# Two early loads issued by ScalarE's queue: a token tile and the scale columns of an adaptive layernorm

## The chip, the cores and the metric

The kernel runs on one core of a Trainium2 chip. A core has TensorE (PE, with its weight loads shown as PEld), VectorE (DVE), ScalarE (ACT), GpSimd (POOL) and SyncE (SP). Each engine works through its own instructions in program order and waits on semaphores for the others. SyncE and ScalarE can issue DMA transfers; each of the two has a queue of its own, and the 16 DMA engines of the core move the data of both. The metric is the device time of one execution in microseconds (us).

## The reference, cut to what matters

A token sequence `x` of 2048 x 512 goes through an attention block and a token-mixing MLP, each behind a layernorm whose scale and shift come from a condition vector `c` of 512 numbers:

```python
mod = (_silu(c) @ w_mod).reshape(c.shape[0], 6, 1, -1)
sa, ca, ga, sb, cb, gb = (mod[:, i] for i in range(6))
h = _layernorm(x, axis=-1) * (1 + ca) + sa
x = x + ga * _A_ref(h, A_wqkv, A_wo)      # sliding, dilated local attention, 32 heads
h = _layernorm(x, axis=-1) * (1 + cb) + sb
x = x + gb * _B_ref(h, B_w1, B_b1, B_w2, B_b2)   # MLP over the token axis
```

`w_mod` is 512 x 3072; its columns 512 to 1023 give `ca`, the scale of the first modulation. All inputs and the output are bf16.

## The kernel before

The 2048 tokens are 16 tiles of 128 rows (`xx[:, st, :]`), worked in chunks of 2, 4, 4, 4 and 2 tiles. Every operation is entered into a graph with a name, an engine (or several to choose from), what it reads and what it writes; then the hand-written list `ORDER` (lines 191 to 248) says in which order they are emitted. Within one engine that order is the order of execution. A suffix such as `:a` picks the engine among an operation's alternatives (a ScalarE, d VectorE, p GpSimd, s SyncE); without one the first alternative is taken. A DMA issue is such an operation too: `dma` (line 374) enters it on SyncE alone.

The change touches the first lines of the list. What is on each engine there, by the names that the prediction uses:

- SyncE issues, in this order: `ld_x0`, `ld_x1` (one x tile of 128 KB each), `ld_x_1_4` and `ld_x_1_2` (two tiles of chunk 1 each, 256 KB), `ld_wmod1` (the scale columns of `w_mod`, 512 KB, into the first `big` buffer), `ld_x_2_8`, `ld_wqkv1` (the k part of the qkv weights, 512 KB), `ld_x_2_6`, `ld_wqkv0`, `ld_wmod0` (shift columns), more x, then `ld_wrow1` (a 384 KB piece of `w_mod`, into `gT`), `ld_b2` and `ld_b1` (bias vectors of 4.0 and 3.5 KB, into `b_t`), and so on.
- ScalarE begins with `act_table` (the load of its function table, line 511) and `ld_c` (line 423), which loads the condition vector `c` (1 KB, 4 rows of 256 bytes) through ScalarE's own DMA queue. Then come the statistics of tile 1 (`ln1s1:a`: two activations with an accumulator over the tile), the reciprocal deviation of chunk 0 (`rstd1_0`), statistics of tile 5, `silu_exp` (the exponential for silu of c), normalizations (`n1_...`), and the four evictions `hT0_...` that multiply the transposed, normalized tokens by the column `a1col`.
- TensorE begins with `cps` (line 528), which transposes `c` into a column; it reads `c_t` and `ident`. Behind it stands `fill:62` (line 521): 15 matmuls of 512 columns and 2 of 128 on the identity, whose result nobody reads. Then `modcols1` (16 matmuls: silu(c) times the scale columns; line 544), the transposes `tr0_0` and `tr1_0`, and `qkv0_10`, the first projection matmul of chunk 0, which needs all four `hT0` columns.
- VectorE does statistics of the other tiles (`ln1s...:d`, aggregated by `ln1v...`), `nb...` (the bias of a normalization), `silu_dve` (makes `sc`, silu of c), some normalizations, and `a1col` (1 + scale, from modcols1's result).
- GpSimd makes constants, and later normalizes tiles and scales weights (`wsc...:p`).

The start of the list, as it is before:

```python
ident act_table halo0 ld_x0 ln1s0:d ln1v0 ld_x1 ld_x_1_4 ld_c cps ln1s1:a ln1v1 rstd1_0 ln1s4:d consts nb1_0 ld_x_1_2
ld_wmod1 fill:62 ln1s5:a ln1v4 ln1s3:d ln1s2:d ld_x_2_8 ld_wqkv1 ln1v3 silu_exp n1_0:a n1_1:p ld_x_2_6 ln1v2 ln1v5
rstd1_1 ld_wqkv0 silu_dve modcols1 nb1_1 n1_3:a n1_4:d tr0_0 n1_2:d n1_5:d a1col wsc1_3:p hT0_2:a tr1_0 ln1s9:d
wsc1_0:p hT0_3:a ln1s8:d ln1v8 ln1s6:d ln1v6 ln1s7:d tr1_2 hT0_1:a hT0_0:a hT1_0:a ln1v9 qkv0_10 ld_wmod0 qkv0_12
```

All instructions are emitted through one wrapper, so the profile puts nearly all of them on line 142; they are told apart by their tiles: `c_t`, `junk<-xx` (statistics on ScalarE), `h<-xx` (normalizations), `psS<-sc,big` (modcols), `psS<-ident` (filler), `hT`, `psS<-hT,wst` (projection).

Of the kernel before, what the change touches and what calls it, by code (L numbers as in the profile page):

```python
# [13 lines left out]
P = 128  # L14
S, D, H, DH, NW, DIL, F = 2048, 512, 32, 16, 8, 2, 1792
# [27 lines left out]
class _Graph:  # L43
# [7 lines left out]
    def add(self, eng, dur, fn, **kw):  # L51
        return self.add_any([(eng, dur, fn)], **kw)
# [136 lines left out]


ORDER = """
ident act_table halo0 ld_x0 ln1s0:d ln1v0 ld_x1 ld_x_1_4 ld_c cps ln1s1:a ln1v1 rstd1_0 ln1s4:d consts nb1_0 ld_x_1_2
ld_wmod1 fill:62 ln1s5:a ln1v4 ln1s3:d ln1s2:d ld_x_2_8 ld_wqkv1 ln1v3 silu_exp n1_0:a n1_1:p ld_x_2_6 ln1v2 ln1v5
rstd1_1 ld_wqkv0 silu_dve modcols1 nb1_1 n1_3:a n1_4:d tr0_0 n1_2:d n1_5:d a1col wsc1_3:p hT0_2:a tr1_0 ln1s9:d
wsc1_0:p hT0_3:a ln1s8:d ln1v8 ln1s6:d ln1v6 ln1s7:d tr1_2 hT0_1:a hT0_0:a hT1_0:a ln1v9 qkv0_10 ld_wmod0 qkv0_12
qkv0_00 hT1_2:a ln1v7 hT1_3:d rstd1_2 nb1_2 ev0_10:a wsc1_2:p ev0_12:d n1_7:a modcols0 sab:a qkv0_02 hT1_1:d ld_x_3_10
ln1s11:a ln1s10:d ln1v10 ld_x_3_12 wsc1_1:p qvb0 qvb_cp0:d ev0_00:a qkv1_13 ld_wrow1 ld_b2 ln1s13:d qkv1_03 ev0_02:a
# [54 lines left out]
def kernel(  # L252
# [31 lines left out]
    nc = _OrderedNC(tc, 1)  # L284
    G = _Graph(dict(ps=6, big=NBIG, vd=NVD))
# [5 lines left out]
    x_view = A_x[0].rearrange("(t p) d -> p t d", p=P)  # L291
# [3 lines left out]
    wmod_view = w_mod.rearrange("(kt p) n -> p kt n", p=P)  # L295
# [7 lines left out]
    def T(shape, dtype, name):  # L303
        return sb.tile(shape, dtype, name=name)
# [10 lines left out]
    xx = T([P, NST, D], BF, "xx")  # L315
# [25 lines left out]
    ident = T([P, P], BF, "ident")  # L341
    group4 = T([P, 32], BF, "group4")
    epscol = T([P, 1], F32, "epscol")
    a1col = T([P, KT], F32, "a1col")
# [19 lines left out]
            ln_t[nm, l] = T([P, NST, n], F32, f"{nm}_{l}")  # L364

    add = G.add

    def copy2(dst, src, n, bf16_src, reads, writes, name, frees=None):
        return G.add_any([("act", _t_act(n), lambda: nc.scalar.activation(dst, src(), ACT.Identity)),
                          ("dve", (0.12 + 0.00052 * n) if bf16_src else _t_tt1(n),  # L370
                           lambda: nc.vector.tensor_copy(dst, src()))], reads=reads, writes=writes, name=name,
                         frees=frees)

    def dma(out_ap, in_ap, nbytes, reads, writes, name, rate=350e3, issue=0.5, lat=2.0, row=1024, **kw):
        return add("sp", issue, lambda: nc.sync.dma_start(*(a() if callable(a) else a for a in (out_ap, in_ap))),
                   reads=reads, writes=writes, name=name, bytes_=nbytes / rate, lat=lat,
                   desc=1 + nbytes // (16 * row), **kw)

    def ln_stats(l, st, src, reads, name):
        st6, mv = ln_t["st6", l], ln_t["mv", l]  # L380

        def fd():
            nc.vector.bn_stats(st6[:, st, :], src)

        def fa():
            nc.scalar.activation(junk[:], src, ACT.Identity, scale=1.0 / D, accum_out=mv[:, st, 0:1])
            nc.scalar.activation(junk[:], src, ACT.Square, scale=D ** -0.5, accum_out=st6[:, st, 0:1])
        o = G.add_any([("dve", 0.68, fd)] + ([("act", 1.26, fa)] if l != 1 else []),
                      reads=reads + (["act_table"] if l == 0 else []), writes=[("stt", l, st)], name=name)

        def fv():
            if o.eng == "dve":
                nc.vector.bn_aggr(mv[:, st, :], st6[:, st, :])
            else:
                nc.vector.scalar_tensor_tensor(mv[:, st, 1:2], mv[:, st, 0:1], mv[:, st, 0:1], st6[:, st, 0:1],
                                               op0=ALU.mult, op1=ALU.subtract, reverse1=True)
        add("dve", 0.15, fv, reads=[("stt", l, st)], writes=[("mv", l, st)], name=name[:3] + "v" + name[4:])
# [16 lines left out]
    def ln_norm(l, g0, n, st, dst, src, reads, writes, name, by_sums=False):  # L414
# [6 lines left out]
    wmodA = big_r[0][:, 0:KT * 2 * D].rearrange("p (k n) -> p k n", k=KT)  # L421
    s_wm = _Slot("big")
    add("act", 0.55, lambda: nc.scalar.dma_start(c_t[:], c[0].rearrange("(t p) -> t p", p=P)), writes=["c_t"],
        name="ld_c", lat=2.0)
    for st in range(SIZES[0]):
        dma(xx[:, st, :], x_view[:, st, :], P * D * 2, [], [("xx", st)], f"ld_x{st}")
    first = None
    for v in (1, 0):
        dma(wmodA[:, :, v * D:(v + 1) * D], wmod_view[:, :, v * D:(v + 1) * D], D * D * 2, [], [("wmodA", v)],
            f"ld_wmod{v}", **(dict(behind=first) if first else dict(alloc=s_wm)))  # L430
        first = first or G.ops[-1]

    wraw = (wst[2][:, 0:KT * D].rearrange("p (k n) -> p k n", k=KT),
# [3 lines left out]
    def ld_w(t):  # L437
        dma(wraw[t], wqkv_view[:, :, t * D:(t + 1) * D], D * D * 2, [], wkey[t], f"ld_wqkv{t}")
# [59 lines left out]
    def halo(ch, nm):  # L498
# [14 lines left out]
        writes=["act_table"], name="act_table")  # L513
# [7 lines left out]
    def fill_fn(k, n):  # L521
# [9 lines left out]
        writes=["ecol"], name="silu_exp")  # L531
# [7 lines left out]
    def f_cols(v):  # L539
# [6 lines left out]
        writes=["a1col"], name="a1col")  # L546
# [62 lines left out]
    def build_chunk(ch):  # L609
# [27 lines left out]
        if ch in XDMA:  # L637
            hX = hT_r[bh][:, 0:KT * C].rearrange("p (s k q) -> p s k q", s=nt, k=KT)
            rhs_of = lambda kt: hX[:, :, kt, :]
            for sl in range(0, nt, XG):  # L640
                st = t0 + sl
# [4 lines left out]
                    writes=[("hTr", ch, sl)] + ([] if sl else [("hT_raw", bh)]), bytes_=0.95, lat=1.2, desc=8,  # L646
                    name=f"xt{st}")
            hkeys = [("hTr", ch, sl) for sl in range(0, nt, XG)]
        else:
            KG = min(KT, 1024 // C)  # L650
            for k0 in range(0, KT, KG):
                s_ = _Slot("ps")

                def f(k0=k0, s_=s_):
# [6 lines left out]
                    name=f"tr{ch}_{k0}")  # L661
# [19 lines left out]
        for (t, j0) in groups:  # L681
            s_ = _Slot("ps")

            def f(t=t, j0=j0, s_=s_):
# [7 lines left out]
                alloc=s_,  # L692
                name=f"qkv{ch}_{t}{j0}")
# [17 lines left out]
            def fd(dst=dst, src=src, bcols=bcols):  # L711
                if GQ == 1:
                    nc.vector.tensor_scalar_add(dst[:, 0, :], src()[:, 0, :], bcols)
                else:
                    nc.vector.tensor_tensor(dst, src(), bcols.unsqueeze(2).to_broadcast([P, GQ, C]), op=ALU.add)
            G.add_any([("act", GQ * _t_act(C, 1), fa), ("dve", _t_tt1(GQ * C), fd)], reads=[("qvb", t)], writes=ekeys,
                      name=f"ev{ch}_{t}{j0}", frees=s_)
# [5 lines left out]
        for dhi in range(4):  # L723
# [3 lines left out]
            def f_vd(s_=s_, dhi=dhi):  # L727
# [5 lines left out]
                writes=[("vD", ch, dhi)], name=f"vd{ch}_{dhi}", lat=1.7, bytes_=P * 4 * (C + PAD) * 2 / 330e3,  # L733
                desc=9, alloc=s_)

        for dlo in range(4):
# [13 lines left out]
            def f(dlo=dlo, prod=prod):  # L750
# [6 lines left out]
                name=f"red{ch}_{dlo}", tiled=True)  # L757
# [15 lines left out]
        def f():  # L773
# [6 lines left out]
            writes=[("lsb", b)], name=f"exp{ch}")  # L780
# [20 lines left out]
        for jj in range(4):  # L801
            G.add_any([(n_, 0.6, lambda jj=jj, q_=q_: q_.dma_start(
                a2sb[:, :, jj * SB:(jj + 1) * SB], ee[32 * jj:32 * jj + 32, :, :]))
                for n_, q_ in (("sp", nc.sync), ("act", nc.scalar))],
                reads=[("lsb", b)], writes=[("a2sb", ba, jj)], name=f"a2_{ch}_{jj}", lat=1.75,
                bytes_=P * 2 * SB * 2 / 150e3, desc=9)

        GO = min(4, GR)
        for q0 in range(0, 4, GO):
            s_ = _Slot("ps")  # L810
            for dq in range(q0, q0 + GO):
# [6 lines left out]
                def f(pv=pv, s_v=s_v):  # L818
# [3 lines left out]
                    name=f"pv{ch}_{dq}")  # L822

                def f(pv=pv, o0=(dq - q0) * C, s_=s_):
# [6 lines left out]
                    name=f"pvacc{ch}_{dq}", tiled=True, **(dict(alloc=s_) if dq == q0 else dict(writes=[s_])))  # L831
# [3 lines left out]
        for st in tiles:  # L835
            s_ = _Slot("ps")

            def f(st=st, s_=s_, res=True):
# [3 lines left out]
                if res:  # L842
# [3 lines left out]
                            alloc=s_, name=f"wo{st}")  # L846
            if st in X1D:
                add("dve", 0.69, lambda st=st, s_=s_: nc.vector.tensor_tensor(xx[:, st, :], ps(s_), xx[:, st, :], op=ALU.add),
                    writes=[("xx", st)], frees=s_, name=f"x1_{st}")
# [7 lines left out]
            def fd(st=st, s_=s_):  # L857
# [3 lines left out]
                      name=f"x1_{st}").link = wo_  # L861
# [9 lines left out]
        for g0 in range(t0, t0 + nt, GRP[ch]):  # L871
# [4 lines left out]
            else:  # L876
                mv = ln_t["mv", 1]

                def f(g0=g0, gn=gn, mv=mv):
# [8 lines left out]
                    writes=[("mv", 1, st) for st in gt], name=f"ln2m{g0}")  # L888
# [5 lines left out]
            def f(g0=g0, gn=gn):  # L894
# [5 lines left out]
                name=f"aff{g0}")  # L900
# [7 lines left out]
    for ch_ in range(NCH):  # L908
        build_chunk(ch_)
# [13 lines left out]
    for s_hi, li, f0, f1, s_lo in sorted(sweeps):  # L923
# [3 lines left out]
        for f_lo in range(f0 * P, f1 * P, EW):  # L927
# [4 lines left out]
            for fl in range(ew // P):  # L932
# [7 lines left out]
                first = True  # L940
                inj = None
                if li in INJ and not last:
# [4 lines left out]
                        name=f"inj{li}_{ft}", alloc=s_)  # L947
                    first = False
                for s0, s1 in zip(steps, steps[1:] + [s_hi]):

                    def f(s_=s_, fl=fl, w1p=w1p, s0=s0, s1=s1, inj=inj, s_lo=s_lo, s_hi=s_hi):
# [4 lines left out]
                        name=f"mlp1_{li}_{ft}_{s0}", **(dict(alloc=s_) if first else dict(writes=[s_])))  # L956
                    first = False
                if li and not inj:
                    if not last:
                        add("dve", 0.69, lambda ft=ft, s_=s_: nc.vector.tensor_tensor(  # L960
                            gT[:, ft, :], ps(s_), gT[:, ft, :], op=ALU.add), writes=[("gT", ft), "gT_use"], frees=s_,
                            name=f"padd{li}_{ft}")
# [7 lines left out]
                else:  # L970
# [4 lines left out]
                              writes=[("gT", ft), "gT_use"], name=f"park{li}_{ft}", frees=s_).link = inj  # L975
# [5 lines left out]
    while s_lo < NST:  # L981
# [13 lines left out]
        for sl in range(ns):  # L995
            st = s_base + sl
# [9 lines left out]
            for hh, (d0, dn) in enumerate(pieces):  # L1006
                s_ = _Slot("ps")
                for ri, (fa, fb) in enumerate(runs):

                    def f(sl=sl, s_=s_, w2p=w2p, d0=d0, dn=dn, fa=fa, fb=fb, hh=hh):  # L1010
# [6 lines left out]
                        name=f"mlp2_{st}_{hh}" + ("" if ri == 0 else "abc"[ri]),  # L1017
                        **(dict(alloc=s_) if ri == 0 else dict(writes=[s_])))

                def f(st=st, s_=s_, d0=d0, dn=dn, hh=hh):  # L1020
# [9 lines left out]
                    writes=okeys,  # L1030
                    name=f"fin{st}_{hh}")
# [37 lines left out]
```

## Time and profile before

| | us |
|---|---|
| median of 3 runs (lowest, highest) | 203.14 (202.55, 203.84) |
| the profiled execution, its own time | 202.81 |
| its span, first to last instruction | 200.9 |
| PE, DVE, ACT, POOL busy in it | 190.1, 159.1, 128.2, 18.1 |
| granted TensorE clock | 1.0 throughout |

The page gives the busy share of each engine in 40 slices of the span and the chain of work that ended last. The timeline lists instructions in order of time, those of one kind merged into one line with a count; SPq and ACTq are the sequencers of SyncE and ScalarE, whose lines here are DMA issues, not transfers. How long a transfer took is in the list of DMA issues, from issue to landing. All engines start their own work at about 0.8 us of the span.

### The profile page before, as it was taken

The page shows a single profiled execution, that of the slowest core. Times are in us where ns is not written, and L with a number is a line of the kernel's source. Part 1 is how long each engine was busy: PE and PEld are TensorE (multiplying, and loading weights), DVE is VectorE, ACT ScalarE, POOL GpSimd, SP SyncE. Part 2 cuts the span into 40 slices and gives each one's busy share as a digit, 9 for nine tenths or more (in the row PEclk, how much of TensorE's full clock was granted, in tenths as well). Part 3 has the DMA queues.
Part 4 walks back from the last instruction along what each step waited for, and adds up shares of the span by engine and source line. Part 5 has one row for each costly group of instructions (what it writes and reads, how often), then busy time and mean ns, then how long its engine had stood idle before and what let it go on. Part 6 is the DMA issues. An engine that isn't in the chain of part 4 may idle for free.

```text
span 200.9 us, 4468 instructions
## 1 busy us (share of the span) xinstructions
PE 190.1 (95%) x1778; PEld 95.1 (47%) x1778; DVE 159.1 (79%) x240; ACT 128.2 (64%) x308; POOL 18.1 (9%) x45
## 2 busy tenths in 40 slices
PE   5989999999898997799999999999999999999993
PEld 1585665444343375334454444444444444444452
DVE  1999999799999999999999899985654420466953
ACT  5889998995898999999999699562660000000000
POOL 4182003000100001010001100510000000000000
PEclk9999999999999999999999999999999999999999
DMA  5999973973709993599963179549910039620121
GB/s 169 330 378 286 304 198 89 208 217 86 259 3 280 291 303 123 172 302 284 237 151 135 31 167 220 157 129 298 337 41 26 26 77 328 211 93 26 52 82 52
DMA packets 53936, 35.94 MB, mean 179 GB/s; under 512 B 24476, under 2 KB 50716, under 8 KB 53916
## 3 DMA queue, kind: packets, MB, share of 16 engines
q1 hardware_dynamic: 52820, 35.50, 62.9%
q8 instruction: 14, 0.23, 0.5%
q10 hardware_dynamic: 1096, 0.17, 0.4%
q14 instruction: 6, 0.05, 0.1%
HBM read 22.55 MB, written 2.10 MB: 123 GB/s over the span
## 4 chain that ended last, share of the span: by engine, by line
PE 66%; ACT 19%; DVE 9%; issue 3%; DMA 1%; SPq 0%; ACTq 0%; DVEq 0%
PE psS L142 64%; ACT junk L142 6%; DVE big L142 5%; ACT v_sb L142 3%; PE psL L142 2%; ACT h L142 2%; DVE h L142 2%; ACT xx L142 1%; ACT o_sb L142 1%; ACT q_sb L142 1%; ACT k_f L142 1%; DMA xx<-in_A_x_dram 1%; ACT hT L142 1%; ACT lv L142 1%; DVE woq L142 1%
## 5 line engine op out<-in xcount | busy, mean ns | idle before, releaser
L142 PEld LDWEIGHTS <-wst 128*128 128x128 bf16 (+1 forms) x482 | 34.9, 101 | 34.8 <-issue 4.5
L142 PE MATMUL psS<-h,wst 128*128 128x512 bf16 (+1 forms) x308 | 51.1, 379 | 0.1
L142 DVE TENSOR_TENSOR big<-a2sb,vD 128x4096 bf16<-128x4096 bf16 (+1 forms) x20 | 36.5, 1856 | 2.0 <-DMA vD<-v_sb 1.3
L142 DVE TENSOR_TENSOR big<-q_sb,k_f 128x4096 bf16<-128x4096 bf16 (+1 forms) x20 | 36.5, 1857 | 0.2 <-ACT q_sb L142 0.2
L142 DVE SCALAR_TENSOR_TENSOR h<-psS,bcol,rows_bc 128x512 f32<-128x512 f32 (+2 forms) x17 | 12.1, 709 | 22.6 <-PE psS L142 22.4
L142 PE MATMUL psS<-hT,w_qkv 128*32 128x512 bf16 (+3 forms) x300 | 29.3, 347 | 0.0
L142 PEld LDWEIGHTS <-w_qkv 128*32 128x32 bf16 (+1 forms) x342 | 19.7, 109 | 16.6 <-issue 3.3
L142 PE MATMUL psS<-gT,big 128*128 128x512 bf16 x112 | 24.8, 379 | 0.0
L142 ACT ACTIVATE junk<-xx 128x512 bf16<-128x512 bf16 x26 | 16.4, 632 | 3.0 <-DMA xx<-in_A_x_dram 1.4
L142 PEld LDWEIGHTS <-big 128*128 128x128 bf16 x144 | 12.0, 97 | 13.2
L142 PE MATMUL psS<-woq,o_sb 128*32 128x512 bf16 (+1 forms) x148 | 16.6, 380 | 0.7 <-ACT o_sb L142 0.7
L142 ACT ACTIVATE gT<-psS,bcol 128x512 bf16<-128x512 f32 x14 | 9.0, 685 | 8.6 <-DVE psS L142 8.4
L142 ACT ACTIVATE h<-xx,nb,rs 128x512 bf16<-128x512 bf16 x16 | 12.7, 812 | 2.4 <-DVE nb L142 2.4
L142 DVE TENSOR_TENSOR psS<-psS,gT 128x512 f32<-128x512 f32 x14 | 9.3, 694 | 6.1 <-PE psS L142 6.1
L142 POOL TENSOR_SCALAR h<-xx,rs,nb 128x512 bf16<-128x512 bf16 x9 | 6.9, 766 | 75.2 <-DVE mv L142 33.1
L142 PE MATMUL psS<-hT,wst 128*128 128x256 bf16 (+2 forms) x88 | 11.7, 343 | 0.8 <-ACT hT L142 0.8
L142 PEld LDWEIGHTS <-group 128*32 128x32 bf16 x288 | 6.5, 95 | 11.0 <-DVE big L142 4.0
L142 DVE TENSOR_TENSOR h<-h,xx 128x512 bf16<-128x512 f32 (+2 forms) x17 | 11.1, 652 | 0.7
L142 PE MATMUL psS<-big,group 128*32 128x512 bf16 (+1 forms) x160 | 9.6, 339 | 2.1 <-DVE big L142 2.0
L142 DVE TENSOR_TENSOR h<-h,rows_bc 128x1024 bf16<-128x1024 bf16 (+2 forms) x16 | 11.0, 690 | 0.4
L142 ACT ACTIVATE q_sb<-psS,qvb 128x512 bf16<-128x512 f32 (+1 forms) x20 | 11.2, 609 | 0.0
L142 ACT ACTIVATE v_sb<-psS,qvb 128x512 bf16<-128x512 f32 (+1 forms) x20 | 10.9, 603 | 0.0
(100 smaller groups left out, 236.5 us busy)
## 6 DMA issues: line engine op xcount, KB each, us to landing
vD<-v_sb SPq DMA_DIRECT2D x12, 524.5 KB, 3.2
big<-in_B_w_dram SPq DMA_DIRECT2D x4, 896.0 KB, 8.9
vD<-v_sb SPq DMA_DIRECT2D x8, 268.5 KB, 3.8
wst<-in_B_w_dram SPq DMA_DIRECT2D x3, 640.0 KB, 5.3
out_dram<-h SPq DMA_DIRECT2D x15, 128.0 KB, 1.7
xx<-in_A_x_dram SPq DMA_DIRECT2D x7, 256.0 KB, 5.9
wst<-in_B_w_dram SPq DMA_DIRECT2D x2, 800.0 KB, 5.2
gT<-in_w_mod_dram SPq DMA_DIRECT2D x4, 384.0 KB, 7.1
```

What stands on the lines that cost most here:

```text
L142: r = fn(*a, **k)
```

## The change

Two transfers get ScalarE's queue as an alternative and are issued there, as ScalarE's first two instructions: `ld_x1` (the second token tile) and `ld_wmod1` (the scale columns of the first modulation). They stand in the list ahead of the table load; `ld_c` keeps its place in the list. The helper `dma2` enters a transfer with both queues as alternatives; the other operations entered through it (`ld_x0`, `ld_wmod0`) have no suffix and stay on SyncE. The last hunk only gives a name to the pair of queues.

```diff
 ORDER = """
-ident act_table halo0 ld_x0 ln1s0:d ln1v0 ld_x1 ld_x_1_4 ld_c cps ln1s1:a ln1v1 rstd1_0 ln1s4:d consts nb1_0 ld_x_1_2
-ld_wmod1 fill:62 ln1s5:a ln1v4 ln1s3:d ln1s2:d ld_x_2_8 ld_wqkv1 ln1v3 silu_exp n1_0:a n1_1:p ld_x_2_6 ln1v2 ln1v5
-rstd1_1 ld_wqkv0 silu_dve modcols1 nb1_1 n1_3:a n1_4:d tr0_0 n1_2:d n1_5:d a1col wsc1_3:p hT0_2:a tr1_0 ln1s9:d
+ident ld_x1:a ld_wmod1:a act_table halo0 ld_x0 ln1s0:d ln1v0 ld_x_1_4 ld_c cps ln1s1:a ln1v1 rstd1_0 ln1s4:d consts
+nb1_0 ld_x_1_2 fill:62 ln1s5:a ln1v4 ln1s3:d ln1s2:d ld_x_2_8 ld_wqkv1 ln1v3 silu_exp n1_0:a n1_1:p ld_x_2_6 ln1v2
+ln1v5 rstd1_1 ld_wqkv0 silu_dve modcols1 nb1_1 n1_3:a n1_4:d tr0_0 n1_2:d n1_5:d a1col wsc1_3:p hT0_2:a tr1_0 ln1s9:d
...
+    QS = (("sp", nc.sync), ("act", nc.scalar))
...
+    def dma2(out_ap, in_ap, nbytes, writes, name, **kw):
+        return G.add_any([(n_, 0.5, lambda q_=q_: q_.dma_start(out_ap, in_ap)) for n_, q_ in QS], writes=writes, name=name,
+                         bytes_=nbytes / 350e3, lat=2.0, desc=1 + nbytes // 16384, **kw)
...
     for st in range(SIZES[0]):
-        dma(xx[:, st, :], x_view[:, st, :], P * D * 2, [], [("xx", st)], f"ld_x{st}")
+        dma2(xx[:, st, :], x_view[:, st, :], P * D * 2, [("xx", st)], f"ld_x{st}")
     first = None
     for v in (1, 0):
-        dma(wmodA[:, :, v * D:(v + 1) * D], wmod_view[:, :, v * D:(v + 1) * D], D * D * 2, [], [("wmodA", v)],
-            f"ld_wmod{v}", **(dict(behind=first) if first else dict(alloc=s_wm)))
+        dma2(wmodA[:, :, v * D:(v + 1) * D], wmod_view[:, :, v * D:(v + 1) * D], D * D * 2, [("wmodA", v)],
+             f"ld_wmod{v}", **(dict(behind=first) if first else dict(alloc=s_wm)))
         first = first or G.ops[-1]
```

More of the change, by code (lines that the diff above doesn't have):

```diff
@@ L803, in build_chunk @@
                 a2sb[:, :, jj * SB:(jj + 1) * SB], ee[32 * jj:32 * jj + 32, :, :]))
-                for n_, q_ in (("sp", nc.sync), ("act", nc.scalar))],
+                for n_, q_ in QS],
                 reads=[("lsb", b)], writes=[("a2sb", ba, jj)], name=f"a2_{ch}_{jj}", lat=1.75,
```

## The prediction

> **What bounds the kernel now.** I read the page first, then the chain that ended last, then the timeline of the first 25 us, then the DMA issues of two short windows and the busy time by stretch.
>
> The page shows TensorE (PE) busy nearly throughout:
>
> ```profile
> PE 190.1 (95%) x1778; PEld 95.1 (47%) x1778; DVE 159.1 (79%) x240; ACT 128.2 (64%) x308; POOL 18.1 (9%) x45
> ```
>
> So at most 10.8 of the 200.9 us are PE idle time, and the chain tells where PE is the bound. Its columns are start, length, what:
>
> ```profile
> 9.82 1.57 ACT hT L142 x4
> 11.40 0.04 issue
> 11.44 8.80 PE psS L142 x108
> ...
> 35.01 5.70 PE psS L142 x80
> 40.71 0.04 DVEq L142
> 40.75 1.52 DVE big L142
> ```
>
> From 11.44 us, where the first projection matmul (qkv0_10) starts, to 40.71 the chain is PE alone. PE has no idle stretch over 0.1 us there; the first is at 52.6. Then the chain goes through VectorE and ScalarE work that PE released, and from 91.4 us it is PE again almost to the end. What moves the start at 11.44 therefore moves the end, unless a later wait has slack against it; none ahead of 40.7 is on the chain. The transfers that stand still in time (the weight and x loads up to 24 us) are no such wait: a later PE finds them landed.
>
> What sets 11.44 is read in the timeline (start, length, engine, operation, tiles, and in brackets the idle time before and its releaser):
>
> ```profile
> 0.81 1.86 SPq L142 DMA_DIRECT2D xx<-in_A_x_dram  x4
> 0.81 1.28 ACT L142 ACT_TABLE_LOAD   x1 [0.81 <-PEq L1053]
> 0.85 0.57 ACTq L142 DMA_DIRECT2D c_t<-in_c_dram  x1
> ...
> 2.50 0.18 PE L142 MATMUL psS<-ident,c_t 4*128 4x4 bf16 x1 [2.50 <-DMA c_t<-in_c_dram]
> ...
> 2.61 5.98 PE L142 MATMUL psS<-ident 128*128 128x512 bf16 x17
> ...
> 2.71 0.47 SPq L142 DMA_DIRECT2D big<-in_w_mod_dram  x1
> ...
> 3.46 0.63 ACT L142 ACTIVATE junk<-xx 128x512 bf16<-128x512 bf16 x1 [1.36 <-DMA xx<-in_A_x_dram]
> ...
> 8.43 0.54 PE L142 MATMUL psS<-sc,big 128*128 128x1 bf16 x16
> ...
> 8.60 1.06 DVE L142 TENSOR_SCALAR h<-xx,rs,nb 128x512 bf16<-128x512 bf16 x3
> ...
> 9.58 0.15 DVE L142 TENSOR_SCALAR a1col<-psS 128x4 f32<-128x4 f32 x1
> ...
> 9.82 2.72 ACT L142 ACTIVATE hT<-psS,a1col 128x256 bf16<-128x256 bf16 x6 [0.41 <-DVE a1col L142]
> ```
>
> The reader is to see PE's own queue: the little transpose of c (cps, 2.50) is released by c's landing; behind it stand the 17 filler matmuls, then the 16 matmuls of modcols1 (8.43). These end at 8.97, but a1col on VectorE stands behind three normalizations until 9.58; then four hT evictions on ScalarE, then 11.44. The filler is cover work today: it occupies 2.61 to 8.43, while VectorE has sc ready at 8.08 (7.92 + 0.16).
>
> **The change, part by part.**
>
> *The second x tile (x1) moves from SyncE's second place to ScalarE's first.* Today it is issued at 1.26 and ScalarE's statistics on it start at 3.46, released by it. The first tile, issued at 0.81, landed at 3.0 (VectorE starts on it at 3.03). So x1 can land at best 0.4 us earlier. But ScalarE's table load (1.28 us) now stands behind two issues. ScalarE's one issue here took 0.57 us; two and the load end at 0.81 + 2 x 0.57 + 1.28 = 3.2. The gain is 0.2 us on ScalarE, at the bounds 0.4 or, if an issue takes longer, about nothing. It is hidden in either case (below); I take 0.
>
> *The scale columns (wmod1, 512 KB) move from SyncE's fifth place (2.71) to ScalarE's second (about 1.4).* Today they land 4.6 us after the issue, at 7.3:
>
> ```profile
> big<-in_w_mod_dram SPq DMA_DIRECT2D x1, 512.0 KB, 4.6
> ```
>
> modcols1 starts at 8.43, when the filler lets it: 1.1 us later. Their earlier landing is worth 0 by itself.
>
> *SyncE's queue.* It loses two issues of about 0.45 us, so x_1_4 moves from 1.72 to 1.26, x_1_2 from 2.20 to 1.72, and what follows by about 1 us. The DMA engines are already full:
>
> ```profile
> 2.50:8.40 5.90, 5.90 (x18) 2.26 (x19) 3.86 (x14) 4.43 (x14) 1.43 (x9) 1.00 0.94 296
> 8.40:11.40 3.00, 2.21 (x43) 1.89 (x42) 2.81 (x9) 2.39 (x6) 0.74 (x2) 1.00 1.08 374
> ```
>
> (The last two columns are the DMA share, 0.94 and 1.08, and GB/s.) Earlier issues thus reorder bytes more than they speed them. x_1_2, now sharing the engines with wmod1, should land at about 6.4 instead of 5.4. VectorE's statistics on it (6.02 to 7.27) then move to about 7.7, and the chunk's rstd and normalizations (8.60 to 9.66) end at about 10.1 to 10.7. This 0.5 to 1 us would be on the path of a1col, if modcols1 stayed at 8.43; it is covered by the next step. From 4.3 us on SyncE's issues also wait for transfers eight places earlier in the list (woq at 11.25 for an x pair that landed at 11.23); the places shift, so wqkv0 would wait for wmod1, but 1 MB is queued ahead of it then: 0. GpSimd issues no DMA here; its first weight scaling waits for a1col and moves with it.
>
> *c moves behind both, on ScalarE's queue.* This is the step that I think decides. Its place in the order list is unchanged, but ScalarE now issues two transfers ahead of it. The issue itself slips from 0.85 to about 2.0, which alone would make c land at 1.6 us later than that, at 3.6. But it is a 1 KB transfer behind 640 KB in one queue. The trace shows such a case on SyncE's queue: the 4 KB of b2, issued at 9.99 right behind 384 KB of w_mod at 9.30:
>
> ```profile
> gT<-in_w_mod_dram SPq DMA_DIRECT2D x1, 384.0 KB, 7.5
> ...
> b_t<-in_B_b_dram SPq DMA_DIRECT2D x1, 4.0 KB, 7.1
> ```
>
> The last column is the time to landing: 9.30 + 7.5 = 16.8 and 9.99 + 7.1 = 17.1. The tiny transfer landed 0.3 us behind the large one ahead of it, after 7.1 us instead of the 1.6 that c took on an empty queue. So c lands when wmod1 does.
>
> When is that? If the two queues get equal shares, 640 KB of ScalarE's and 640 KB of SyncE's (x0, x_1_4, x_1_2) have moved by then: the same 1,280 KB that today have moved when wmod1 lands. Bounds: ScalarE's queue served alone at 374 GB/s from 2.0 us, where data begins to flow: 0.655 MB take 1.75 us, c at 3.8. No gain over today's: 7.3, and a little more if SyncE's queue is favoured. Equal halves: 1.31 MB at 374 GB/s give 5.5, at the 296 GB/s of that same stretch 6.4. I take 6.4, because the nearest row (the same loads, the same time) has that rate. c is then 6.4 - 2.45 = 3.95 us late.
>
> The Trainium skill (DMA: Bandwidth & Descriptors, "Queues, rings and completion order") says that each DMA engine takes turns between the queues that have work for it, packet by packet. By that rule the halves are equal and the sum is the one taken here. No row of this trace shows two loaded queues, so it stays untested until the run.
>
> *What stands behind c.* cps, the 17 fillers and modcols1 are in order on PE. Filler time is 8.43 - 2.50 = 5.93 us from cps to modcols1, whenever it starts: the cover is gone, because the filler now begins at 6.5 and nobody else needs it. modcols1 starts at 6.4 + 0.05 + 5.93 = 12.4. Its first 11 matmuls stand 0.43 us apart, the others 0.22 (the change comes at 7.28), so all slow it would be 15 x 0.427 + 2 x 0.107 = 6.6 us, all fast 15 x 0.216 + 2 x 0.056 = 3.4. I take the measured time, since PE comes from idleness in both cases.
>
> The Trainium skill (TensorE: Matmul & The Clock Gate, "Part 1") has a free-running window of 3.4 us of activity after which the clock opens. By that rule the slow stretch lasts 3.4 to 6.8 us, the filler 5.0 to 6.6, and the sum below would be +2.8 to +4.4 instead of +3.6. The 4.7 us of slow spacing seen here lie inside that.
>
> Behind cps on other engines: ScalarE's silu_exp (7.09 today) needs cps at 6.65, so no more than today.
>
> *Given back.* From modcols1 to 11.44 are 3.01 us today. Then VectorE has its normalizations done and a1col no longer stands behind them: a1col ends at +0.75; the transposes that the first hT reads end at +1.01 (0.41 + 8 x 0.055, and latency 0.2); hT starts at +1.06, takes 1.58 and 0.04 to PE: +2.68. So 0.33 us come back.
>
> **Sum:** +3.95 (c) + 0 (filler, same length) - 0.33 = +3.6 us at 11.44, so 15.0, and at the end. The profiled execution took 202.81 us (span 200.9, 1.9 around it): 206.4. The median of the runs is 203.14, 0.33 above the profiled one: I predict 206.7. Ends: c at 3.8 gives +1.0 (204.1), c at 7.6 gives +4.8 (207.9).
>
> **Rivals.**
>
> *c is not held up by the data ahead of it* (its four small packets pass, or the queues are served in another order). Then only the issue order costs: c at 3.6 at most, modcols1 at 9.6, +0.8 after the 0.33 given back; 204.0, or 203.6 if the issue slips by 0.8 only. Not slower by over 1%. For it: c uses few packets. Against it: b2's 7.1 us. It decides where c lands before about 4.8 us. Chance 0.10.
>
> *The filler shortens.* If PE's slow spacing ended at a fixed time (7.28) and not after so much activity, the late filler would have 2 slow matmuls and 15 fast ones, 3.7 us instead of 5.8: +1.5, 204.7. Only one PE start from idle is in the trace, so nothing excludes it. Chance 0.08.
>
> *The gain that the loads could bring.* x1 up to 0.4 us earlier moves ScalarE's statistics, rstd, normalizations and a1col: -0.4 at most, 202.8, if c is not late. It needs the first rival and, besides, a filler that is not pushed back; VectorE's x_1_2, later by up to 1 us, speaks against it. Chance 0.02; even then it is not over 1%.
>
> *Slack later.* DVE and ACT are at 98% and more from 60 to 90 us, and everything there is released by work that moved; but if half of the shift were absorbed before 91.4, +1.8: 204.9. The 1.3 us that VectorE waits for a vD transfer and PE's 3.9 us of gaps up to 91 speak for it, that they lie behind shifted work against. Chance 0.06.
>
> *c later than 7.6:* SyncE's queue is served first; 208 to 210. Chance 0.04.
>
> **How the numbers follow.** The forecast (c between 5.3 and 7.6, +2.5 to +4.8) has 0.70; its own range is 205.6 to 207.9. To hold 8 in 10 the range reaches down to 204.6, which takes in the shortened filler and the absorbed half, and up to 208.0. A measurement of this kernel can tell about 1% (2 us) from no change: faster by that 0.01 (half of the third rival), within it 0.22 (the first two, the rest of the third, half of the fourth), slower 0.77.
>
> **What would show it.** Right: the wait of cps for c ends at 5.5 to 7.4 instead of 2.50, wmod1 lands about then too; the fillers start right behind; modcols1 near 12.4, a1col 0.6 behind it, the first qkv matmul near 15, the chain from there unchanged and shifted. Wrong: cps at 3.6 or before; fillers 0.22 apart from the start; or the first qkv matmul late and PE's gaps between 50 and 91 us smaller by the same amount.

## The result, and the profile after

The changed kernel is slower: 205.88 us as the median of 5 runs (204.29 to 207.53) against 202.84 (201.59 to 203.84); the ratio is 1.0122, 95% interval 1.0082 to 1.0163, so about +2.5 us. (The medians are over all runs; this ratio and those below leave out runs that were over 1.5% above the fastest of the same kernel.) A second set of runs gave 1.0103 (1.0068 to 1.0138). The profiled execution took 204.89 us with a span of 202.9, 2.0 more than before.

The page after, busy time by engine; VectorE's and ScalarE's work is the same to 0.3 us, so the time is waiting:

```profile
PE 189.0 (93%) x1763; PEld 95.2 (47%) x1778; DVE 159.0 (78%) x240; ACT 128.5 (63%) x308; POOL 18.1 (9%) x45
```

The chain that ended last, first 52 us (start, length, what):

```profile
1.79 3.94 DMA c_t<-in_c_dram
5.73 0.05 issue
5.78 7.45 PE psS L142 x42
13.23 0.02 issue
13.25 1.58 ACT hT L142 x4
14.83 0.04 issue
14.87 5.03 PE psS L142 x66
...
38.45 5.70 PE psS L142 x80
44.15 0.04 DVEq L142
44.19 0.03 issue
44.22 1.22 DVE woq L142
```

Before, the transfer of tile x1 and its statistics on ScalarE opened the chain:

```profile
1.26 2.17 DMA xx<-in_A_x_dram
...
3.46 0.73 ACT junk L142 x2
```

The transfer of c now stands there, with 3.94 us. Behind it come 7.45 us of PE (transpose of c, filler, modcols1), the hT evictions, and the first projection matmul at 14.87 instead of 11.44. The same in the timeline:

```profile
0.82 0.42 ACTq L142 DMA_DIRECT2D xx<-in_A_x_dram  x1
...
1.27 0.46 ACTq L142 DMA_DIRECT2D big<-in_w_mod_dram  x1
...
1.79 0.63 ACTq L142 DMA_DIRECT2D c_t<-in_c_dram  x1
...
3.61 0.63 ACT L142 ACTIVATE junk<-xx 128x512 bf16<-128x512 bf16 x1 [0.57 <-DMA xx<-in_A_x_dram]
...
5.78 0.18 PE L142 MATMUL psS<-ident,c_t 4*128 4x4 bf16 x1 [5.78 <-DMA c_t<-in_c_dram]
...
5.89 6.48 PE L142 MATMUL psS<-ident 128*128 128x512 bf16 x17
...
12.20 0.54 PE L142 MATMUL psS<-sc,big 128*128 128x1 bf16 x16
...
12.78 0.16 DVE L142 TENSOR_SCALAR a1col<-psS 128x4 f32<-128x4 f32 x1 [2.45 <-PE psS L142]
```

c lands at 5.73 (issued at 1.79), the filler starts right behind and ends 6.4 us later; VectorE sits idle 2.45 us for PE ahead of a1col; before, it came to a1col from its normalizations without a pause. x1 gained nothing: its statistics start at 3.61 instead of 3.46.

Not all of the 3.43 us of the start reach the end. The place where some are lost is in VectorE's products with `vD`, a tile into which SyncE's queue copies the attention's values from `v_sb`; VectorE multiplies it with the attention weights in `a2sb`. Instruction by instruction, VectorE is 3.43 us later than before from 16 us on, and 2.04 later from one place near 39 us to the end. Before, in VectorE's timeline (the last two lines follow without idle time, so VectorE itself sets when they start):

```profile
34.04 3.49 DVE L142 TENSOR_TENSOR big<-a2sb,vD 128x2048 bf16<-128x2048 bf16 x3
38.84 1.23 DVE L142 TENSOR_TENSOR big<-a2sb,vD 128x2048 bf16<-128x2048 bf16 x1 [1.31 <-DMA vD<-v_sb]
39.98 2.28 DVE L142 TENSOR_TENSOR big<-q_sb,k_f 128x4096 bf16<-128x4096 bf16 x1
42.18 1.22 DVE L142 TENSOR_TENSOR woq<-woq,rows_bc 128x2048 bf16<-128x2048 bf16 x1
```

and after, the four in one go:

```profile
37.48 4.62 DVE L142 TENSOR_TENSOR big<-a2sb,vD 128x2048 bf16<-128x2048 bf16 x4
```

The fourth product waited 1.31 us for its vD transfer before, and does not after: 1.39 us are given back there. The list of DMA issues has that transfer with the time from issue to landing at the end, before:

```profile
vD<-v_sb SPq DMA_DIRECT2D x1, 268.5 KB, 4.8
```

and after:

```profile
vD<-v_sb SPq DMA_DIRECT2D x1, 268.5 KB, 3.1
```

### The profile page after: what moved, and what is told of

It reads as the page before. It is cut to its first block, busy times and chain, and to the rows that moved or that the text cites. A ratio compares the mean times of both kernels' runs of the same rounds, so it can differ in the third digit from the quotient of the medians.

```text
span 202.9 us, 4453 instructions
## 1 busy us (share of the span) xinstructions
PE 189.0 (93%) x1763; PEld 95.2 (47%) x1778; DVE 159.0 (78%) x240; ACT 128.5 (63%) x308; POOL 18.1 (9%) x45
## 4 chain that ended last, share of the span: by engine, by line
PE 55%; DVE 18%; ACT 18%; issue 4%; DMA 2%; ACTq 1%; DVEq 0%
PE psS L142 53%; DVE big L142 12%; ACT junk L142 6%; DVE h L142 3%; ACT v_sb L142 3%; ACT h L142 3%; DMA c_t<-in_c_dram 2%; PE psL L142 2%; ACT k_f L142 1%; ACT o_sb L142 1%; ACT q_sb L142 1%; ACT xx L142 1%; ACTq L142 1%; DVE st L142 1%; ACT hT L142 1%
## 5 line engine op out<-in xcount | busy, mean ns | idle before, releaser
L142 PE MATMUL psS<-woq,o_sb 128*32 128x512 bf16 (+1 forms) x145 | 15.9, 380 | 1.3 <-ACT lv L142 1.0
L142 DVE TENSOR_TENSOR h<-h,xx 128x512 bf16<-128x512 f32 (+2 forms) x17 | 11.1, 652 | 0.7
L142 DVE BATCH_NORM_STATS2 st<-xx 128x6 f32<-128x512 bf16 x12 | 8.0, 681 | 4.1 <-DMA xx<-in_A_x_dram 4.0
## 6 DMA issues: line engine op xcount, KB each, us to landing
vD<-v_sb SPq DMA_DIRECT2D x8, 268.5 KB, 3.0
```

Source lines behind the costliest of these rows:

```text
L142: r = fn(*a, **k)
```

## The experiments

The theory: c stands behind the transfers that ScalarE issues ahead of it, the filler stands behind c on PE, and this sets the first projection matmul. The main rival: the reordering of the large loads and the later table load cost the time, and c's lateness is hidden. A second question came from the profile after: whether the missing vD wait belongs to the change.

**Only c late.** The kernel before, with c issued by SyncE behind the scale columns:

```diff
-    add("act", 0.55, lambda: nc.scalar.dma_start(c_t[:], ...
+    add("sp", 0.55, lambda: nc.sync.dma_start(c_t[:], ...
-... ld_x1 ld_x_1_4 ld_c cps ln1s1:a ...   ld_wmod1 fill:62
+... ld_x1 ld_x_1_4 ln1s1:a ...            ld_wmod1 ld_c cps fill:62
```

> The kernel before with one edit: c is issued by SyncE right behind the scale columns, so that only c is late; no other load moves to another queue. Theory: c lands at about 7.4 to 7.6, the filler runs from there, modcols1 at 12.5 to 13.8, first projection matmul at 15.2 to 16.5, time +2.5 to +4.5 us on before, more than the change itself costs. Rival (c's lateness is hidden, the moved loads cost it): 0.

Measured: 1.0201 (1.0175 to 1.0228), +4.1 us, with no load moved. Its timeline:

```profile
7.85 0.18 PE L142 MATMUL psS<-ident,c_t 4*128 4x4 bf16 x1 [7.85 <-DMA c_t<-in_c_dram]
...
7.96 6.45 PE L142 MATMUL psS<-ident 128*128 128x512 bf16 x17
...
14.83 0.16 DVE L142 TENSOR_SCALAR a1col<-psS 128x4 f32<-128x4 f32 x1 [4.16 <-PE psS L142]
...
16.91 1.25 PE L142 MATMUL psS<-hT,wst 128*128 128x256 bf16 x10 [0.76 <-ACT hT L142]
```

c was 5.35 us later than before, the first projection matmul 5.47 later (somewhat more than expected, through a longer filler). A late c alone is sufficient for the loss, and a later c costs more.

**The filler ahead of the transpose of c**, all loads as in the change:

```diff
-... ld_x_1_4 ld_c cps ...          nb1_0 ld_x_1_2 fill:62
+... ld_x_1_4 ld_c fill:62 cps ...  nb1_0 ld_x_1_2
```

> As after, but the filler matmuls stand ahead of the transpose of c on TensorE instead of behind it; c still lands behind the 640 KB. Theory: the filler runs from 1.45 to between 7.2 and 7.9, the transpose of c follows with c landed at 5.7 long before, sc is ready at 8.9 as after, modcols1 at about 9.0, first projection matmul at 12.1: +0 to +0.7 us on before. So c may be late if nothing long stands behind it. Rival (reordered loads cost it): as after, +2 to +3 us.

Measured: 1.0033 (0.9998 to 1.0067), not told from before.

```profile
1.44 5.13 PE L142 MATMUL psS<-ident 128*128 128x512 bf16 x17 [1.44 <-POOL epscol L142]
...
6.50 0.17 PE L142 MATMUL psS<-ident,c_t 4*128 4x4 bf16 x1
...
11.91 1.36 PE L142 MATMUL psS<-hT,wst 128*128 128x256 bf16 x11 [0.83 <-ACT hT L142]
```

The transpose of c runs at 6.50, later still than after, and the matmul comes at 11.91, 0.47 later than before; by as much the normalizations are late (they end at 10.13 instead of 9.66), since x_1_2 lands later. So at the start the late c costs nothing once the filler no longer waits for it: it is the filler behind c that is paid for. This place of the filler may have another price. In nine of the twelve executions the mean granted clock was 0.98 to 0.99, and they took 203.6 to 206.3 us; the other three, the profiled one among them, had 0.997 or more and took 202.7 to 203.1. In the profile PE is idle for 2.20 us ahead of modcols1; whether that goes with the lower clock is not shown.

**Half the filler**, `fill:62` to `fill:31`, in the changed kernel.

> As after, with 31 instead of 62 units of filler (7 matmuls of 512 columns and 3 of 128). Theory (the filler behind the late c is what is waited for): it ends at about 9.2, a1col then waits for the normalizations (10.3) and not for TensorE, first projection matmul at 12.1 to 13, since TensorE may still be on its slow spacing then; time +0.5 to +1.8 us on before. Rival (something else sets the start): as after, +2 to +3 us.

Measured: 0.9973 (0.9946 to 0.9999): not slower, and just below the kernel before. c is as late as ever:

```profile
5.57 0.18 PE L142 MATMUL psS<-ident,c_t 4*128 4x4 bf16 x1 [5.57 <-DMA c_t<-in_c_dram]
...
5.68 3.49 PE L142 MATMUL psS<-ident 128*128 128x512 bf16 x10
...
8.96 0.61 PE L142 MATMUL psS<-sc,big 128*128 128x1 bf16 x16
...
12.04 2.78 PE L142 MATMUL psS<-hT,wst 128*128 128x256 bf16 x24 [0.82 <-ACT hT L142]
```

The start is right for the theory (12.04), the time is a miss, lower than the +0.5 us or more that were expected: the vD wait near 38 us was 0.02 us in this profile. The same edit in the kernel before tells whether the filler is a cost by itself:

> The kernel before with 31 instead of 62 units of filler and no load moved. The halved filler made the changed kernel 0.3% faster than before. Theory (it does so by what it leaves out behind a late c, and by where the instruction fetch falls): here c is on time, the normalizations set a1col at 9.6 as before, first projection matmul at 11.4 to 11.8, time -1 to +0.5 us, with the VectorE wait near 39 us present or absent as the fetch falls. Rival (the filler is a cost of its own, whatever stands ahead of it): -0.5 us at the first projection matmul.

Measured: 0.9989 (0.9962 to 1.0015). The first projection matmul came at 11.89, 0.45 later than before (modcols1 waited for the scale columns until 8.77, and the transposes behind it took 2.72 us instead of 1.78), and the vD wait was 0.19 us. So the filler is no cost by itself where c is on time: with half of it the start came later, not 0.5 us earlier as the rival has it.

**c first on ScalarE's queue**, then x1 and the scale columns:

```diff
-ident ld_x1:a ld_wmod1:a act_table ... ld_x_1_4 ld_c cps
+ident ld_c ld_x1:a ld_wmod1:a act_table ... ld_x_1_4 cps
```

> The condition vector c is issued first on ScalarE's queue, ahead of the second token tile and the scale columns; all else as after. Theory (c's place behind 640 KB decides, through the filler behind it): the transpose of c starts at 2.5 again, the filler ends at about 8.4, and what is left of the cost is the later x_1_2 (landed at 6.84 after, 5.36 before): normalizations end at 10.3, first projection matmul at 12.1 (11.44 before, 14.87 after). Time 0 to +0.7 us on before. Rival (the reordered loads and the later table load cost the time, c's lateness is hidden): first projection matmul at 14 or later, time +2 to +3 us.

Measured: 1.0070 (1.0039 to 1.0100), +1.4 us: a miss for the theory, which said 0 to +0.7 us, and for the rival, which said +2 to +3.

```profile
0.82 0.57 ACTq L142 DMA_DIRECT2D c_t<-in_c_dram  x1
...
1.43 0.37 ACTq L142 DMA_DIRECT2D xx<-in_A_x_dram  x1
...
2.23 0.18 PE L142 MATMUL psS<-ident,c_t 4*128 4x4 bf16 x1 [2.23 <-DMA c_t<-in_c_dram]
...
4.98 0.63 ACT L142 ACTIVATE junk<-xx 128x512 bf16<-128x512 bf16 x1 [1.39 <-DMA xx<-in_A_x_dram]
...
9.65 0.54 PE L142 MATMUL psS<-sc,big 128*128 128x1 bf16 x16 [2.04 <-DVE sc L142]
```

c is on time (2.23) and PE done early, but x1, now issued at 1.43 behind SyncE's x_1_4 (1.27), lands at 4.96. ScalarE's statistics start 1.52 us late, and everything down to the first projection matmul (12.97) is 1.53 late. The order of the large loads is thus a cost of its own, as the rival said, though a smaller one. In the change x1 goes first and is not late in this way.

**One load at a time.** Only x1 on ScalarE (the scale columns back on SyncE), and only the scale columns:

```diff
+ident ld_x1:a act_table ...      # only_x1;  ld_wmod1 back behind ld_x_1_2
+ident ld_wmod1:a act_table ...   # only_wmod1;  ld_x1 back behind ln1v0
```

> Only the second token tile is issued by ScalarE; the scale columns stay on SyncE. Theory: c stands behind 128 KB alone and lands at about 3.6, the filler ends at 9.5 to 10, first projection matmul at 12.2 to 12.7, time +0.5 to +1.2 us on before. Rival (reordered loads): x_1_2 is not behind the scale columns any more, so 0.

> Only the scale columns are issued by ScalarE; the second token tile stays on SyncE. Theory: c stands behind 512 KB, lands at about 5.0 (5.73 after), modcols1 at about 11.1 to 11.5, first projection matmul at 13.8 to 14.2, time +1.5 to +2.5 us on before. Rival (reordered loads): as after, with c's landing of no account.

Only x1: 0.9992 (0.9963 to 1.0021). c landed at 3.57 as expected, but the filler took 5.0 us instead of 5.8 and the first projection matmul came at 11.62; the expected +0.5 us or more did not come (the shorter filler was luck), and this run does not tell the theories apart. Only the scale columns: 1.0075 (1.0049 to 1.0100), +1.5 us. c landed at 4.64, the filler took 5.0 us, and modcols1 came at 9.92, well before the 11.1 that were expected:

```profile
5.25 0.63 ACT L142 ACTIVATE junk<-xx 128x512 bf16<-128x512 bf16 x1 [2.65 <-DMA xx<-in_A_x_dram]
...
9.92 0.54 PE L142 MATMUL psS<-sc,big 128*128 128x1 bf16 x16
...
10.40 1.06 DVE L142 TENSOR_SCALAR h<-xx,rs,nb 128x512 bf16<-128x512 bf16 x3
...
11.37 0.15 DVE L142 TENSOR_SCALAR a1col<-psS 128x4 f32<-128x4 f32 x1
```

a1col stood behind the normalizations, and these were late because x1 on SyncE landed at 5.23: the 512 KB had gone ahead of it. The first projection matmul came at 13.24. The size in time was as expected, but not the cause: it was the late x1.

**c between the two loads** (`ident ld_x1:a ld_c ld_wmod1:a act_table`):

> Both loads stay on ScalarE's queue, but c is issued between them: tile x1, then c, then the scale columns. Theory (c's place behind the 512 KB, and the filler behind c, make the loss): c lands at about 3.6 as with x1 alone ahead of it, the filler ends between 8.7 and 9.6, x1 keeps its early landing (3.6), x_1_2 stays late (6.8), so the normalizations end at about 10.3 and the first projection matmul comes at 11.9 to 12.3 (14.87 after). Time +0 to +0.8 us on before. Rival (the scale columns ahead of the x tiles, or the later table load, cost it): +2 to +3 us.

Measured: 1.0057 (1.0031 to 1.0084), +1.2 us, somewhat over what was expected. In its profile c lands at 3.7, the transpose is at 3.78, x1's statistics at 3.63; x_1_2 lands at 7.14 (6.84 after, 5.36 before) and the normalizations end at 10.64; the matmul comes at 12.42. So with c moved up by one place about half of the loss in time goes, and most of it at the start; the rest is x_1_2, which moved at the same time as the scale columns (these landed at 8.82).

**The two kernels once more**, for a second profile each:

> The changed kernel once more, for a second profile. Theory: transpose of c at 5.5 to 6, filler 5 to 6.6 us long by where the slow spacing of the matmuls ends, first projection matmul at 13.8 to 15.2, time +1.5 to +3.3 us. VectorE's wait for the last vD transfer near 40 us: if the missing wait of the first profile was an accident of that execution, there is a wait of 0.8 to 1.8 us again, and the shift of the start is passed on in full; if a late start always removes it, no wait, and 1 to 1.5 us less than the shift of the start.

> The kernel before once more, for a second profile. Theory (the wait of VectorE near 39 us comes from a 16 KB instruction fetch that delays one of the 16 DMA engines of the vD transfer when it starts less than about 2.3 us after that transfer is issued): a wait of 0.8 to 1.8 us at the fourth vD product if the fetch starts by then, none if later. Rival (the wait comes from the transfer's own size and the traffic): a wait of 1.3 us, and all 16 engines late. Filler 5.0 to 6.6 us, first projection matmul at 11.4 to 11.6, ratio 1.00.

After again: 1.0103, c at 6.19, the first projection matmul at 15.31, no vD wait. Before again: 1.0005 (0.9973 to 1.0037), 11.46, and a vD wait of 1.18 us. So the wait was there in both profiles of before and in neither of after. Each transfer has 16 landing marks in the trace, as many as there are DMA engines. In all 13 profiles, 15 marks of the vD transfer came by 3.0 to 3.2 us after its issue. What differs is the last mark, and a 16 KB packet of the kind "instruction" (the profile lists it under q8; the expectations call it an instruction fetch) that runs beside the transfer for 0.9 to 1.4 us:

| start of the instruction packet after the vD issue, us | last mark, us after the issue | wait of VectorE, us | profiles |
|---|---|---|---|
| 1.17 to 2.27 | 4.06 to 4.78 | 0.81 to 1.81 | 9, among them both of before |
| 2.30 to 2.73 | 3.02 to 3.20 | 0 to 0.19 | 4: both of after, both with half the filler |

The 15 other marks were on time in both rows, which speaks against the rival of that expectation (size and traffic). In the nine of the first row the last mark came 1.55 to 1.72 us behind the end of the instruction packet, wherever that fell, which speaks for the theory. No run moved the packet on purpose.

**The version that the runs point to**, only x1 on ScalarE and the filler ahead of the transpose of c:

> The version that the runs point to: only the second token tile on ScalarE's queue, and the filler ahead of the transpose of c on TensorE. Theory: c lands at 3.6 and waits for the filler (to 6.3 to 7.9), silu of c is ready at about 8.1 to 8.5, the normalizations end at 9.8, first projection matmul at 11.6 whatever the filler's length; time -0.5 to +0.5 us on before.

Measured: 1.0005 (0.9976 to 1.0034), first projection matmul at 11.79, vD wait 1.81 us. It loses nothing and gains nothing. The change with half the filler, 0.9973, is the best of these kernels, by 0.5 us and at the edge of its interval.

## Why the prediction was right

The measured 205.88 lies within the range of 204.6 to 208.0, and up to the first projection matmul the mechanism is the one that was forecast. By its own steps:

- *c waits for the data ahead of it in ScalarE's queue: right.* It landed at 5.73, and 3.94 us after its issue instead of 1.60. The rival that it would pass them fell. It did not quite wait for all of the scale columns: their last part landed at 6.12, in the second profile at 7.15 with c at 6.19.
- *1,280 KB ahead of it, equal halves, 6.4 us: mis-sized by 0.7 us* (by 0.2 in the second profile). The two queues did not mix evenly. In the stretch from 4 to 5 us of the changed kernel, packets by queue (q10 is ScalarE's, q1 SyncE's; a packet is one row of 1 KB here):

```profile
q10 hardware_dynamic: 345, 0.34, 98.3%
q1 hardware_dynamic: 30, 0.02, 6.8%
```

  The scale columns went through almost alone, then x_1_2. So nearer 1,024 KB were ahead of c (x0, x1, x_1_4, the scale columns) than 1,280. This is no rule, however: with c between the loads, the scale columns and x_1_2 moved side by side from 5 to 7 us:

```profile
q10 hardware_dynamic: 351, 0.36, 58.7%
q1 hardware_dynamic: 297, 0.29, 42.0%
```

  The prediction weighed the Trainium skill here (DMA: Bandwidth & Descriptors, "Queues, rings and completion order": each DMA engine takes turns between queues, a packet of typically 9 to 17 descriptors, at most 64, at a time). A sixteenth of the scale columns is 32 rows of 1 KB, so a turn as long as that is within the page's ceiling and above what it calls typical; the records do not say which engine moved what, so the length of a turn is not shown. What is shown is that equal halves held in one run and not in another.
- *The filler takes as long as before, 5.93 us to modcols1: mis-sized by 0.5.* It took 6.42, since 14 of its matmuls stood about 0.43 us apart, and before 11, with a twelfth at 0.39. The two errors nearly cancelled, which is luck: modcols1 at 12.20, predicted 12.4.
- *0.33 us given back from modcols1 to the first projection matmul: right*, 2.67 us instead of 3.01. (The terms in the prediction's bracket for the transposes add up to 1.05, not 1.01; hT started 1.05 behind modcols1, against the 1.06 of the sum.)
- *Sum at the start, +3.6: right*, +3.43 in the first profile, +3.87 in the second.
- *"and at the end": the term that failed.* The prediction passed the whole shift on to the end; of the 3.43 us, 2.04 reached it. The prediction named the 1.3 us of VectorE's vD wait among what could be absorbed, and gave it 0.06. It read the chain as PE alone up to 40.71; VectorE's 1.31 us of idle time at 38.84 stood beside that chain, and it was VectorE that set the start of the work from 42 us on. The other runs bear this out. In each of the 11 profiles of other kernels or of after, VectorE's shift against the first profile of before stays the same to 0.1 us from 16 us on, except at this place, where it changes by the difference of the two waits, to 0.1 us. With half the filler VectorE is 0.6 us late at 16 us and 0.7 early from there to the end; with c first it is 1.5 late and then 2.0. That the wait is gone goes with where an instruction packet falls (the table above); that the late start puts it there is not shown: with c still later, in the run with only c late, the wait was 1.58 us. The second profile of before has one more such place. There a third of the qkv weights (loaded into `h`) landed at 20.54, and PE waited for it:

```profile
20.58 0.69 PE L142 MATMUL psS<-sab,h 128*128 128x1 bf16 x16 [0.66 <-DMA h<-in_A_wqkv_dram]
```

  The prediction's "no such wait" ahead of 24 us thus holds for the profile that it read and not for this one. Between the two second profiles the start is 3.85 us later and VectorE's end 1.7: 1.3 went at the vD wait and 0.9 ahead of it, most of that at this one.
- *x1 worth 0, the table load hidden, x_1_2 covered: right in sum.* x_1_2 landed at 6.84 (6.4 predicted), the normalizations ended at 10.33 (10.1 to 10.7). c_first and the run with c between the loads show what the order of the loads costs by itself: 1.0 to 1.5 us at the first projection matmul. The 1.1 us by which modcols1 came behind its scale columns was one execution's: they landed at 7.34, and at 8.53 and 8.72 in the other two profiles with the loads of before, where modcols1 did wait for them. With the full filler that cost nothing, since a1col stood behind the normalizations (9.58 and 9.59).

The forecast was 206.7, the median 205.88. In the ratio, +1.2% against the +1.8% that was forecast, it is "and at the end" that makes most of the difference. (Among the signs of slack, ScalarE is not busy for 98% from 60 us on: 9.43 of the 10 us up to 70.)

## What to carry to other kernels

A transfer of 1 KB took its place in the queue's line here, small as it was: before putting large loads at the head of a queue, look for the small one that is issued behind them, and for what stands behind its reader. Work that only fills time must stand where its start doesn't depend on anything late: the same filler behind the waiting instruction put 3 us on the first projection matmul, ahead of it none (what it may cost in granted clock there is open). And a shift at the start is not a shift at the end until the idle time of every engine, not only of the one on the chain, has been looked at on the way.

## What the runs showed of the hardware that was not expected

- Two loaded queues did not always share evenly: one could have the DMA engines nearly to itself for a microsecond. In the run with only the scale columns on ScalarE, from 3 to 4 us:

```profile
q10 hardware_dynamic: 364, 0.37, 105.4%
q1 hardware_dynamic: 10, 0.01, 2.2%
```

  An x tile issued on the other queue 0.45 us after the 512 KB landed at 5.23 instead of 3.44. In the run with c between the loads the queues did share; what decides is open.
- The slow spacing of PE's matmuls (0.427 us for 512 columns, 0.216 afterwards) lasted 2.7 us in one profile of the kernel before and 4.7 in the other; it was 6.0 in all three profiles in which the full filler began after 5.8 us. The full filler, from its first matmul's start to its last's, took 4.6 to 6.3 us. The Trainium skill (TensorE: Matmul & The Clock Gate, "Part 1") has a free-running window of 3.4 us, and says that one kernel runs 6, 11 or 14 slow matmuls by where in that window it starts. The 6 and 11 matmuls at full slow spacing in the two profiles of before and the 14 of the late starts agree with that; the 2.7 us are shorter than one window. Why the late starts were all long is open.
- Where a 16 KB instruction packet began 1.17 to 2.27 us after a 268.5 KB transfer was issued, the last of the transfer's 16 landing marks came 0.9 to 1.7 us behind the others, and VectorE waited for it (9 profiles); where it began at 2.30 us or later, neither (4 profiles).
